# Fewer steps of the weights' conversion in the first batch row of an attention and mixer kernel

## The chip, the core and the metric

The kernel runs on one core of a Trainium2 chip. The metric is the device time of one execution in microseconds (us); 1392.67 us is the median of seven runs before the change (1392.23 to 1396.2). Engine names are those of the profile: PE is the matrix engine, PEld its weight load, DVE the vector engine, ACT the scalar engine, POOL the GpSimd engine, SP the sync engine; SPq and ACTq are DMA issues from SP and ACT.

## The reference

Eight batch rows; in each, eight heads of 576 tokens and width 64. Attention keeps only scores close to the row's maximum, then a mixer follows, first over tokens, then over channels.

```python
scores = q @ k.T / 8                                   # (8, 8, 576, 576)
scores = where(scores >= max(scores) - tau, scores, -1e9)
attn = exp(scores - max); attn /= sum(attn) + 1e-9
x = (attn @ v) -> (8, 576, 512)                        # heads side by side
u = x + (relu(x.T @ w_tok1) @ w_tok2).T                # 576 -> 256 -> 576
out = u + relu(u @ w_ch1) @ w_ch2                      # 512 -> 1536 -> 512
```

The four weights arrive in 64-bit floating point, the rest in 32 bits. The kernel computes in 32 bits, so it must convert the weights on the chip first.

## The kernel before

**Units.** The work on attention is cut into 144 units, 18 for each batch row. A unit is 128 query tokens of a pair of heads (the fifth of every nine units has instead the last 64 tokens of two pairs). One iteration `u` of the main loop does several stages for different units: `scores(u)` (PE, L301) with the row maximum on DVE (`mx`, L306) and the bias on POOL (L307); `norm(u - 1)` (DVE L330, L331; POOL L334); the transposes of the weights of unit `u - 2`; `weigh(u)` (ACT: L316, then the exponential L323); and `values` (PE, L408 and L413, tiles `pv`), every second unit or so.

In batch row 0 the transposes are made on PE (L357, tiles `tr`) and copied out by DVE or ACT (L359, tiles `eT`). In later rows DVE transposes 32 x 32 blocks (L368, tile `T`) and 16 DMAs on SP's queue put the blocks in place (L378, `eT<-T`), one such group for two units, or for the shared unit.

**The mixer.** When a batch row's attention is done, its mixer is pushed to a list of small steps; `fill(share)` takes steps from it into the following row's units, a fixed cost per unit. So rows 1 to 7 have attention and mixer matmuls in one PE queue, and row 0 has attention alone. The steps are: transposes of x (L430), the token mixer (L439, L446, with DVE's addition L450), the channel mixer's first product `ch1` (L468, into a double-buffered PSUM tile that ACT's relu L469 empties) and its second `ch2` (L480, L484).

**The weights' conversion.** The weights come in 31 pieces: 0 to 2 are `w_tok1`, 3 to 6 `w_tok2`, 7 to 18 `w_ch1`, 19 to 30 `w_ch2`. A piece is loaded by SP (L176) into one of four raw buffers, and converted by two ACT instructions (L191, L193), three DVE instructions (L201, L205, L209) and one POOL addition (L215). `weight(n)` issues the next `n` of 94 steps:

```python
for k in range(steps_done, min(steps_done + n, 3 * len(pieces) + 1)):
    i, part = divmod(k, 3)
    if part == 0:
        on_gpsimd(i - 1)
        if i:
            load_piece(i - 1 + NRAW)
    else:
        on_scalar(i + 1, part - 1)
    on_vector(i, part)
```

So each step has one DVE instruction. Every third step has besides the POOL addition of the piece before, and the load of the piece three ahead, which needs the raw buffer that this addition has just read. The two others have an ACT instruction for the next piece. The order on every engine is the program's order; nothing is reordered.

`weight` is called in an iteration after `scores` and `norm` (rows after 0 only), ahead of `weigh(u)`, and behind `weigh(u)`. Row 0 takes the last two calls, and the rows after it take two steps in all three calls, until the 94 are done. `need(i)` issues steps early if a mixer step wants piece `i` and it hasn't been issued.

The loads of q and k (L106) are on SP's queue in row 0 and on ACT's in later rows; v (L114) is always on SP's. `prep` (DVE L283) transposes q and k of a pair of heads.

Of the kernel before, what the change touches and what calls it, by code (L numbers as in the profile page):

```python
# [21 lines left out]
def kernel(  # L22
# [144 lines left out]
    def load_piece(i):  # L167
        if i >= len(pieces):
            return
        dst, src = pieces[i]  # L170
        rows = dst.shape[0]
        n = 1
        for d in dst.shape[1:]:
            n *= d
        raw = raw_at[i % NRAW][0:rows, 0 : n * (2 if wide(i) else 1)].bitcast(src.dtype)
        nc.sync.dma_start(out=like(raw, dst), in_=src)  # L176
        if wide(i):
            words = raw.bitcast(U32).rearrange("p (n w) -> p n w", w=2)
            h2 = work.tile([P, WMAX], F32, tag="o", name=f"h2_{i}")[0:rows, 0:n]
            raws[i] = like(words[:, :, 0], dst), like(words[:, :, 1], dst), like(h2, dst)  # L180
        else:
            raws[i] = like(raw, dst)
# [4 lines left out]
    def on_scalar(i, part):  # L187
        if wide(i):
            lo, hi, h2 = raws[i]
            if part == 0:  # L190
                nc.scalar.activation(out=lo.bitcast(I32), in_=lo, func=AF.Copy, scale=2.0**-29)  # L191
            else:
                nc.scalar.activation(out=h2, in_=hi.bitcast(F32), func=AF.Square)  # L193

    def on_vector(i, part):
        if wide(i):
            dst = pieces[i][0]
            lo, hi, h2 = raws[i]
            bits = dst.bitcast(U32)
            if part == 0:  # L200
                nc.vector.tensor_scalar(  # L201
                    out=bits, in0=hi, scalar1=3, scalar2=0x3FFFFFFF, op0=ALU.logical_shift_left, op1=ALU.bitwise_and
                )
            elif part == 1:
                nc.vector.scalar_tensor_tensor(  # L205
                    out=bits, in0=hi, scalar=0xC0000000, in1=bits, op0=ALU.bitwise_and, op1=ALU.bitwise_or
                )
            else:
                nc.vector.scalar_tensor_tensor(out=dst, in0=h2, scalar=2.0**-30, in1=dst, op0=ALU.is_ge, op1=ALU.mult)  # L209

    def on_gpsimd(i):
        if i >= 0:
            dst = pieces[i][0]
            if wide(i):
                nc.gpsimd.tensor_tensor(out=dst.bitcast(I32), in0=dst.bitcast(I32), in1=raws.pop(i)[0].bitcast(I32), op=ALU.add)  # L215
            else:
                nc.gpsimd.tensor_copy(out=dst, in_=raws.pop(i))
# [5 lines left out]
    def weight(n):  # L223

        nonlocal steps_done
# [9 lines that stand above are left out]
            steps_done = k + 1  # L235
# [39 lines left out]
    def in_blocks(b):  # L275
        return b > 0
# [10 lines left out]
    def scores(u):  # L287
        b, p0, t = units[u]
        sc = [
            (ps_3rd if b == 0 and (2 * u + h) % 3 == 2 else ps_sc).tile([P, 2, MAIN], F32, tag="sc", name=f"sc{h}_{u}") for h in range(2)  # L290
        ]
        if t == SHARED:
            parts = [(b * NP + p0 + i, slice(MAIN, S), slice(64 * i, 64 * i + 64)) for i in range(2)]
        else:
            i, c = divmod(t - (t > SHARED), NI)
            parts = [(b * NP + p0 + i, slice(P * c, P * c + P), slice(0, P))]
        order = [(f, part, h) for f in range(2) for part in parts for h in range(2)]
        for f, (n, cols, rows), h in order if b else sorted(order, key=lambda o: o[2]):
            r = slice(D * h, D * h + D)
            qT, kT = heads[n]  # L300
            nc.tensor.matmul(sc[h][rows, f, 0:HS], lhsT=qT[r, cols], rhs=kT[r, HS * f : HS * f + HS], start=True, stop=True)  # L301
        mx = small.tile([P, 2], F32, tag="mx", name=f"mx_{u}")
        bias = small.tile([P, 2], F32, tag="bias", name=f"bias_{u}")
        for h in range(2):
            c = slice(h, h + 1)
            nc.vector.tensor_reduce(out=mx[:, c], in_=sc[h][:, :, 0:HS], axis=AX.XY, op=ALU.max)  # L306
            nc.gpsimd.tensor_scalar(out=bias[:, c], in0=mx[:, c], scalar1=toff, scalar2=-SCALE, op0=ALU.add, op1=ALU.mult)  # L307
        st[u] = sc, bias
# [18 lines left out]
    def norm(u):  # L327
        e, rs = st[u]
        rr = small.tile([P, 2], F32, tag="rr", name=f"rr_{u}")
        nc.vector.tensor_scalar(out=rr, in0=rs, scalar1=1e-9, scalar2=None, op0=ALU.add)  # L330
        nc.vector.reciprocal(out=rr, in_=rr)  # L331
        for h in range(2):
            eh = e[:, S * h : S * h + S]
            nc.gpsimd.tensor_scalar(out=eh, in0=eh, scalar1=rr[:, h : h + 1], scalar2=1.0, op0=ALU.mult, op1=ALU.mult)  # L334
        st[u] = e

    def group_of(u):

        b, p0, t = units[u]
        if t == SHARED:  # L340
            return (b, p0, "s"), 0, 1
        i, c = divmod(t - (t > SHARED), NI)
        return (b, p0 + i, c // 2), c % 2, 2
# [17 lines left out]
    def turn_blocks(u):  # L361

        key, place, n = group_of(u)
        e = st.pop(u)
        if place == 0:
            Ts[key] = work.tile([P, NK * 2 * P], F32, tag="T", name=f"T_{u}")
        T = Ts[key][:, 0 : NK * n * P]
        nc.vector.transpose(  # L368
            out=T.rearrange("p (a c n x) -> p c a n x", a=4, c=NK, n=n)[:, :, :, place, :],
            in_=e.rearrange("p (c a x) -> p c a x", c=NK, a=4),  # L370
        )
        if place == n - 1:
            del Ts[key]
            eTs[key] = work.tile([P, NK * 2 * P], F32, tag="eT", name=f"eT_{u}")
            w = NK * n * 32
            for a in range(4):
                for i in range(4):
                    nc.sync.dma_start(  # L378
                        out=eTs[key][32 * a : 32 * a + 32, w * i : w * i + w], in_=T[32 * i : 32 * i + 32, w * a : w * a + w]
                    )  # L380
# [151 lines left out]
    b_now = 0  # L532
    LAG = 2
    for u in range(len(units) + LAG + 4):
        on = u < len(units)
        if u == UB:
            late.close()
            ps_mm = ctx.enter_context(tc.tile_pool(name="ps_mm", bufs=2, space=bass.MemoryType.PSUM))
        if on:
            b_now, p0, t = units[u]  # L540
            n = b_now * NP + p0
        w = u - LAG
        back = 0 <= w < len(units)
        if on:
            scores(u)
        if 0 < u <= len(units):
            norm(u - 1)
        if b_now:
            weight(2)
        if back:  # L550
            key, place, many = group_of(w)
            if in_blocks(key[0]):
                turn_blocks(w)
            else:
                for i in range(3):
                    turn(w, i)
            if place == many - 1:
                b, p, c = key
                if c == 0 and p % 2 == 0:
                    split_middle(b * NP + p)  # L560
                if c == "s":
                    split_middle(b * NP + p + 1)
                when = u + (2 if in_blocks(b) else 1)
                due += [(when, b, p + i, c) for i in range(2 if c == "s" else 1)]
        if b_now:
            fill(0.4)
        weight(2 if b_now else 1)
        if on:
            weigh(u)
        elif b_now:  # L570
            fill(0.6)
        weight(2 if b_now else 1)
        if on:
            m = n + 2 + t // 4
            if t < 8 and m < len(pairs):
                load_qk(m, (nc.scalar if b_now else nc.sync,) * 2, t % 4)
                if t % 4 == 3:
                    load_v(m)
            if t == 2:
                prep(n + 1)  # L580
            if t == 7 and n + 2 < len(pairs):
                prep(n + 2)
        while due and due[0][0] <= u:
            _, b, p, c = due.popleft()
            values(b, p, c)
            if p == NP - 1 and c == 1:
                push(b)
# [31 lines left out]
```

## Time and profile before

| | |
|---|---|
| median of 7 runs | 1392.67 us (1392.23 to 1396.2) |
| the profiled execution's own time, and its span | 1393.08 us, 1391.3 us |
| mean granted PE clock | 0.989 |
| PE busy | 1327.6 us (95%), 6866 matmuls |
| DVE, ACT, POOL busy | 585.9 us, 590.5 us, 359.3 us |
| chain that ended last | PE 86%, DVE 6%, DMA 2%, POOL 2%, SPq 2% |
| DMA | 128.34 MB, mean 92 GB/s |

A busy share is an average over stages with different limits. In the profile's picture of 40 slices (34.8 us each) PE is under 90% in the first five slices only. The first scores start at 8.1 us, row 1's first scores at 101.3 us, the first mixer matmuls at 125.5 us, and the last conversion instruction of the weights is POOL's at 197.7 us.

### The profile page before, as it was taken

To read this page: it belongs to the slowest core of one execution; us is meant where nothing else is said; L and a number is where in the kernel's file an instruction comes from. 1 tells how busy PE (TensorE), PEld (TensorE's weight loads), DVE (VectorE), ACT (ScalarE), POOL (GpSimd) and SP (SyncE) were. 2 spreads that over 40 slices of the span, in tenths; PEclk is the share of its full clock that TensorE was granted. 3 is DMA by queue.
4 is the path that set the end of the run, shared out by engine and by line. 5 is a ranking of instruction groups with operands and counts; after the bars stand their busy time and mean duration, and the time that the engine had idled before them with its cause. 6 is when DMAs were issued, how large, how long until landed. Compare 5 with 4: busy or idle time off the path is not lost.

```text
span 1391.3 us, 19515 instructions
## 1 busy us (share of the span) xinstructions
PE 1327.6 (95%) x6866; PEld 831.3 (60%) x6866; DVE 585.9 (42%) x1009; ACT 590.5 (42%) x1328; POOL 359.3 (26%) x683
## 2 busy tenths in 40 slices
PE   5776899999999999999999999999999999999998
PEld 3443465646565566665766567565657566575675
DVE  5789784444444444434243344433333453101000
ACT  5776564544454444443434435353434444120110
POOL 4566563232222222212222222221221222000000
PEclk9997999999999999999999999999999999999999
DMA  6354754443444434433434444443433433300000
GB/s 131 91 121 115 196 139 122 110 119 92 109 116 107 106 86 99 109 83 79 110 84 93 102 96 102 99 104 80 98 92 89 102 77 85 84 8 16 8 8 23
DMA packets 257376, 128.34 MB, mean 92 GB/s; under 512 B 208064, under 2 KB 221376, under 8 KB 257280
## 3 DMA queue, kind: packets, MB, share of 16 engines
q1 hardware_dynamic: 131632, 111.46, 30.5%
q10 hardware_dynamic: 125648, 15.64, 7.1%
q8 instruction: 55, 0.90, 0.3%
q14 instruction: 41, 0.34, 0.1%
HBM read 43.25 MB, written 9.44 MB: 38 GB/s over the span
## 4 chain that ended last, share of the span: by engine, by line
PE 86%; DVE 6%; DMA 2%; POOL 2%; SPq 2%; ACT 1%; issue 1%; ACTq 0%; DVEq 0%; POOLq 0%
PE c L484 27%; PE c L468 26%; PE sc L301 11%; PE pv L413 7%; PE t L439 5%; PE t L446 3%; DVE mx L306 3%; PE pv L408 2%; SPq L378 2%; PE tx L430 1%; PE c L480 1%; PE pv_s L413 1%; DVE T L368 1%; DMA scratch<-in_moe_w_ch_dram 1%; POOL e L334 1%
## 5 line engine op out<-in xcount | busy, mean ns | idle before, releaser
L306 DVE TENSOR_REDUCE mx<-sc 128x1 f32<-128x576 f32 x288 | 204.7, 752 | 525.2 <-PE sc L301 523.2
L468 PE MATMUL c<-xT,wc 128*128 128x256 f32 (+1 forms) x1920 | 399.0, 361 | 1.5 <-ACT g L469 1.4
L484 PE MATMUL c<-wc,g 128*128 128x512 f32 x864 | 389.1, 596 | 0.0
L468 PEld LDWEIGHTS c<-xT,wc 128*128 128x128 f32 x1920 | 334.2, 190 | 71.3 <-issue 28.0
L307 POOL TENSOR_SCALAR bias<-mx,toff 128x1 f32<-128x1 f32 x288 | 80.1, 278 | 814.1 <-DVE mx L306 757.9
L316 ACT ACTIVATE e<-sc,bias 128x576 f32<-128x576 f32 x288 | 199.3, 740 | 158.0 <-POOL bias L307 157.7
L484 PEld LDWEIGHTS c<-wc,g 128*128 128x128 f32 x864 | 157.9, 190 | 175.2 <-issue 173.2
L469 ACT ACTIVATE g<-c 128x256 f32<-128x256 f32 (+1 forms) x240 | 86.9, 362 | 334.3 <-PE c L468 326.9
L334 POOL TENSOR_SCALAR e<-e,rr 128x576 f32<-128x576 f32 x288 | 219.7, 776 | 15.8 <-DVE rr L331 3.8
L323 ACT ACTIVATE e<-e,ntau 128x576 f32<-128x576 f32 x288 | 220.6, 771 | 0.0
L301 PE MATMUL sc<-kT,qT 64*128 64x288 f32 (+1 forms) x1280 | 190.7, 435 | 13.4 <-DVE kT L283 8.1
L368 DVE STREAM_TRANSPOSE T<-e 128x1152 f32<-128x1152 f32 x126 | 172.5, 1369 | 16.2 <-DMA eT<-T 10.0
L301 PEld LDWEIGHTS sc<-kT,qT 64*128 64x128 f32 (+1 forms) x1280 | 103.9, 180 | 90.3 <-issue 47.9
L413 PE MATMUL pv<-eT,lv 128*64 128x256 f32 x1024 | 125.6, 389 | 0.0
L413 PEld LDWEIGHTS pv<-eT,lv 128*64 128x64 f32 x1024 | 75.7, 141 | 39.3 <-issue 4.1
L418 ACT COPY xT<-pv 128x256 f32<-128x256 f32 x64 | 23.8, 372 | 162.0 <-PE pv L413 154.3
L489 DVE COPY o<-c 128x512 f32<-128x512 f32 x36 | 24.5, 680 | 160.8 <-PE c L484 160.8
L446 PE MATMUL t<-w,a 128*128 128x288 f32 x256 | 78.0, 433 | 12.7 <-DVE xT L450 9.6
L439 PE MATMUL t<-x_sb,w 128*128 128x512 f32 x160 | 72.6, 600 | 0.7 <-ACT g L469 0.7
L446 PEld LDWEIGHTS t<-w,a 128*128 128x128 f32 x256 | 46.1, 194 | 40.3 <-DVE xT L450 17.5
L450 DVE TENSOR_TENSOR xT<-xT,t 128x288 f32<-128x288 f32 x64 | 27.9, 440 | 80.4 <-PE t L446 80.2
L323 ACT ACTIVATION_READ_ACCUMULATOR e<-e,ntau 128x1 f32 x288 | 56.4, 196 | 0.0
(48 smaller groups left out, 602.7 us busy)
## 6 DMA issues: line engine op xcount, KB each, us to landing
eT<-T SPq DMA_DIRECT2D x896, 72.0 KB, 2.0
scratch<-in_moe_w_ch_dram SPq DMA_DIRECT2D x24, 512.0 KB, 4.0
lv<-in_v_dram SPq DMA_DIRECT2D x32, 288.0 KB, 3.4
out_dram<-o SPq DMA_DIRECT2D x36, 256.0 KB, 2.2
eT<-T SPq DMA_DIRECT2D x224, 36.0 KB, 1.9
lk<-in_k_dram ACTq DMA_DIRECT2D x108, 72.0 KB, 2.7
lq<-in_q_dram ACTq DMA_DIRECT2D x104, 72.0 KB, 2.1
lq<-in_q_dram SPq DMA_DIRECT2D x24, 72.0 KB, 3.4
```

The costliest lines, as they stand in the source:

```text
L301: nc.tensor.matmul(sc[h][rows, f, 0:HS], lhsT=qT[r, cols], rhs=kT[r, HS * f : HS * f + HS], start=True, stop=True)
L306: nc.vector.tensor_reduce(out=mx[:, c], in_=sc[h][:, :, 0:HS], axis=AX.XY, op=ALU.max)
L316: nc.scalar.activation(out=eh, in_=sc[h][:, :, 0:HS], func=AF.Prelu, bias=bias[:, h : h + 1], scale=SCALE, alpha=STEEP)
L323: nc.scalar.activation(out=eh, in_=eh, func=AF.Exp, bias=ntau, accum_out=rs[:, h : h + 1])
L334: nc.gpsimd.tensor_scalar(out=eh, in0=eh, scalar1=rr[:, h : h + 1], scalar2=1.0, op0=ALU.mult, op1=ALU.mult)
L368: nc.vector.transpose(out=T.rearrange("p (a c n x) -> p c a n x", a=4, c=NK, n=n)[:, :, :, place, :], in_=e.rearrange("p (c a x) -> p c a ...
L413: nc.tensor.matmul(to[r], lhsT=lv[:, j, :], rhs=eT[:, j], start=False, stop=(c == NI - 1), skip_group_check=True)
L439: nc.tensor.matmul(ps, lhsT=w1[:, t, P * m : P * m + P], rhs=x_sb[:, t, :], start=(t == 0), stop=(t == NT - 1))
L446: nc.tensor.matmul(ps, lhsT=s["a"][:, m, P * c : P * c + P], rhs=w2[:, m, HS * f : HS * f + HS], start=(m == 0), stop=(m == NTK - 1))
L468: nc.tensor.matmul(ps, lhsT=wc1[:, j, c, :], rhs=uT[:, c, GR * i : GR * i + n], start=(c == 0), stop=(c == NCC - 1))
L469: nc.scalar.activation(out=s["g"][:, j, 0:n], in_=ps, func=AF.Relu)
L484: nc.tensor.matmul(flat, lhsT=s["g"][:, j, P * t : P * t + P], rhs=wc2[:, j, :], start=False, stop=(j == NJ - 1), skip_group_check=True)
```

## The change

One call of `weight` changes, the one ahead of `weigh(u)`. In row 0 it issued one step in each of the 18 units; now it issues one in units 0, 3, 6, 9, 12 and 15 (`u % 3 == 0` is a truth value, which counts as 1 or 0). The call behind `weigh(u)` still issues one step per unit.

```diff
         if b_now:
             fill(0.4)
-        weight(2 if b_now else 1)
+        weight(2 if b_now else u % 3 == 0)
         if on:
             weigh(u)
         elif b_now:
             fill(0.6)
         weight(2 if b_now else 1)
```

Row 0 so ends with 24 steps issued instead of 36: pieces 0 to 7 have their DVE instructions behind them, not pieces 0 to 11. Rows after 0 still issue six steps per unit. The 94th step is issued in unit 29 instead of unit 27. PE's instructions stand in the same order in both kernels.

## The prediction

> **What bounds the kernel now.** I read the picture of 40 slices first, to see where PE has room at all.
>
> ```profile
> PE   5776899999999999999999999999999999999998
> DVE  5789784444444444434243344433333453101000
> ```
>
> PE is full from the sixth slice on, so an edit is worth what it changes before about 200 us: the time is the moment at which PE is full, plus a queue of matmuls whose order doesn't change. In slices 3 and 4 DVE is the busiest engine. The chain of waits runs in row 0 (8 to 101 us) through PE's scores, DVE's maximum, DVE's copies `eT` and back to PE; between 101 and 185 us it also passes POOL's addition L215, a load into the raw buffers and ACT's L191; from 190 us it is PE alone.
>
> Next, DVE's timeline in row 0 (start, duration, what it did, in brackets the idle time before it). The scores of unit 15 take PE from 86.25 to 87.50.
>
> ```profile
> 83.56 1.42 DVE L306 TENSOR_REDUCE mx<-sc 128x1 f32<-128x576 f32 x2 [2.39 <-PE sc L301]
> ...
> 86.83 0.68 DVE L205 SCALAR_TENSOR_TENSOR wc<-scratch,wc 128x512 uint32<-128x512 uint32 x1
> 87.54 0.69 DVE L209 SCALAR_TENSOR_TENSOR wc<-h,wc 128x512 f32<-128x512 f32 x1
> 88.16 1.41 DVE L306 TENSOR_REDUCE mx<-sc 128x1 f32<-128x576 f32 x2
> ```
>
> Unit 14 has `pv` matmuls ahead of its scores, and DVE idles 2.39 us: conversion there is free. Unit 15 has none; two steps stand ahead of its maximum, which starts 0.6 us late. So a removed step is worth nothing in half of the units.
>
> Then SP's queue and ACT's timeline where the conversion ends.
>
> ```profile
> 165.57 2.69 SPq L176 DMA_DIRECT2D scratch<-in_moe_w_ch_dram  x2
> 168.36 11.01 SPq L378 DMA_DIRECT2D eT<-T  x16
> 179.48 1.50 SPq L176 DMA_DIRECT2D scratch<-in_moe_w_ch_dram  x3
> ```
> ```profile
> 183.49 0.68 ACT L191 ACTIVATE scratch<-scratch 128x512 int32<-128x512 uint32 x1 [4.83 <-DMA scratch<-in_moe_w_ch_dram]
> ...
> 186.30 1.37 ACT L316 ACTIVATE e<-sc,bias 128x576 f32<-128x576 f32 x2
> ```
>
> The loads of pieces 28 to 30 stand behind 16 block DMAs (unit 24's group), whose issue takes 11 us. ACT waits 4.83 us for the first, and the scores of unit 26 (PE, 180.03) reach ACT's L316 only at 186.30. PE loses just 0.97 us, since three `ch1` and a `pv_s` lie between the scores of units 26 and 27.
>
> **Row 0: the gain.** Out of it go 12 steps of 512 columns: by rows such as those above 4 x (0.42 + 0.69 + 0.69) = 7.2 us of DVE, 4 x 1.3 us of POOL, 8 x 0.67 us of ACT (0.55 us apart) and four loads. 7.2 us would be the gain if DVE ended last everywhere. What is on the path:
> - Units 1 to 4. ACT's L193 (16.34) no longer stands ahead of unit 1's L316 (16.90): 0.55 us. At 22.97 L205 and L209 (1.32 us) stand ahead of `prep` and unit 3's maximum (25.65), whose scores are ready at 24.07; one L201 (0.42) takes their place. Iteration 3 then runs the two wider instructions itself (1.37 for 1.1 us). I take 0.8 us of these.
> - Unit 6: L191 (39.53) ahead of L316, and L209 (0.88) ahead of the maximum: 0.6 us.
> - Units 9 and 13: 0.1 us each (maxima at 57.47 and 77.53 against scores ready at 57.28 and 77.11; iteration 12 keeps two steps, but of 288 columns). Unit 15: 0.6 us.
> - Iteration 17: L191 (100.70) delays L316 to 101.27, and with it the scores of unit 18; DVE then has two steps ahead of the maximum at 103.86. Of 0.55 us on ACT and 1.0 us on DVE I take 0.8.
>
> Sum 3.0 us; at least 1.5 (units 9, 13, 15, 18 alone).
>
> **Units 18 to 26: moved as a block.** They run six steps each as before, on pieces numbered four lower, with the same three raw buffers filled ahead, so I move them by the gain. One difference: the load ahead of L191 at 131.53 is then of `w_ch1`; an earlier one of those landed 3.65 us after its issue (109.15), this one took 4.19: 0.5 us more gain. In all -3.5 us.
>
> **Units 27 to 29: the loss.** The 12 DVE steps come back here. As DVE work they cost nothing: PE ends last, and DVE, 45% busy from 200 us, is then as full as it is now in units 25 to 27. Were that cover gone, mx of unit 29 would be some 2 us late. What costs is the order on SP. Pieces 27 to 30, loaded by 181 us before, are now issued in iterations 26 and 27, so that pieces 28 to 30 fall behind unit 26's group of block DMAs. In the times of before:
>
> ```profile
> 184.27 1.97 POOL L334 TENSOR_SCALAR e<-e,rr 128x576 f32<-128x576 f32 x2
> 186.22 3.23 POOL L215 TENSOR_TENSOR wc<-wc,scratch 128x512 int32<-128x512 int32 x2
> ```
>
> That group starts at 186.34. Ahead of it now stands the load of piece 27, which waits for iteration 26's first addition (186.22 + 1.6 = 187.85, as at 165.57 above, where the second load and the group waited for L215): group at 188.35. It takes 10.05 to 11.0 us: load of piece 28 at 198.4 to 199.4, landed 4.0 us later (179.48 to 183.49), at 202.4 to 203.4. ACT has it next, at the end of iteration 27, and reaches it at 196. Behind it on ACT are L193, piece 29's pair, a relu and then unit 28's L316: 2.6 us as in 183.49 to 186.30 (less a copy), so L316 starts at 205.0 to 206.0 instead of 199.16. It empties the scores' PSUM tiles, 0.65 and 1.35 us later.
>
> ```profile
> 195.67 1.24 PE L301 MATMUL sc<-kT,qT 64*128 64x288 f32 x8
> 196.84 3.72 PE L468 MATMUL c<-xT,wc 128*128 128x256 f32 x16
> 200.49 0.65 PE L408 MATMUL pv<-eT,vl 128*64 128x256 f32 x4
> 200.98 1.90 PE L413 MATMUL pv<-eT,lv 128*64 128x256 f32 x16
> 202.80 1.24 PE L301 MATMUL sc<-kT,qT 64*128 64x288 f32 x8
> ```
>
> Here only 7.1 us of matmuls lie between two units' scores. Unit 29's can start at 205.7 and end at 207.3 to 208.3, not 204.04: 3.2 to 4.2 us, I take 3.7. The later steps then have room: unit 29's L316 ends by 212.7 where PE wants the buffers at 214, and `ch2` wants piece 30 at 218 where POOL is done by 216.
>
> **The clock.** That leaves PE empty for about 2.8 us. The two nearest gaps in the trace:
>
> ```profile
> 116.17 0.90 PE L357 MATMUL tr<-ident,e 128*128 128x128 f32 x3 [2.58 <-DVE eT L359]
> ...
> 167.08 2.21 PE L446 MATMUL t<-w,a 128*128 128x288 f32 x8 [2.33 <-DVE xT L450]
> ```
> ```profile
> 116.00:118.00 2.00, 1.82 (x7) 0.50 0.00 0
> 118.00:120.00 2.00, 2.00 (x10) 0.50 0.22 69
> 120.00:122.00 2.00, 2.00 (x12) 0.50 1.13 296
> ```
>
> In the windows (PE busy, matmuls, granted clock) the gap of 2.58 us is followed by 6.6 us at half clock, the one of 3.04 us (107.13) by 3.3, the one of 2.28 (31.83) by 5.5, and the one of 2.33 at 167.08 by none. Half clock costs half of its length where PE is the bound: 0 to 3.3 us. I take 2.5, from the mean of the first two, which are nearest.
>
> The Trainium skill ("TensorE: Matmul & The Clock Gate", HAM oscillation) puts the limit at idle gaps above about 3.4 us. By it 2.8 us would cost no clock and the sum would be +0.2; this trace shows the drop after shorter gaps.
>
> **Sum.** -3.5 + 3.7 + 2.5 = +2.7 us on 1393.08 us, the profiled execution's own time, which is 0.4 us above the median: 1395.4 us as a median. A difference of 0.2% (2.8 us) is about what a measurement of this kernel can tell from no change.
>
> **Rivals.**
> - *The wait finds cover, and the kernel is faster.* If piece 28 lands by 199 us (3.4 us sooner), L316 of unit 28 ends in time for unit 29's scores at 202.80, PE has no gap, and row 0's gain stays: -3.5, 1389.2 us. For it: the same wait of ACT at 183.49 cost PE 0.97 us. Against it: the 2 us of matmuls fewer in unit 28, and the 16 issues, which never took under 10 us between 137 and 190 us. Below this, row 0 could give up to 7.2 us.
> - *The wait without the clock's drop.* As after 167.08: +0.2, 1392.9 us.
> - *Row 0 gives less.* If only units 9, 13, 15 and 18 count, 1.5 us come in, the loss of 6.2 stays: +4.7, 1397.4 us. For it: at the start PE, DVE, ACT and POOL wait for each other, and a gain at one is lost at the next.
> - That the change doesn't do what it says is not open: 18 + 6 = 24 steps by the loop, and the orders on the engines show pieces 0 to 7 ahead of row 1.
>
> **How the numbers follow.** The sum above: 0.50, its own range 1393.4 to 1397.4 by the bounds of wait and clock, so half of it on each side of +0.2%. Covered wait: 0.22, nearly all faster. No drop: 0.13, nearly all the same. Small gain: 0.15, slower. That makes faster 0.22, same 0.38, slower 0.40. The range runs from the covered wait to the small gain with the longer stall: 1388.9 to 1398.6.
>
> **What would show it.** Right: row 1's first scores near 98 us instead of 101.3; seven loads in SP's queue from 179 us on, less the gain, three of them behind the group of unit 26; ACT's L191 waiting 6 us for a load ahead of unit 28's L316; a PE gap of 2 to 4 us ahead of unit 29's scores, with windows of clock 0.5 after it. Wrong: no such gap; row 1's first scores at 101 us; or units 18 to 26 taking longer or shorter than before (with unit 27, 94.3 us from 101.33 to 195.67), which would mean that they don't move as a block.

## The result, and the profile after

The changed kernel takes 1396.29 us (median of 16 runs, 1394.78 to 1401.39) against 1393.08 us before (39 runs beside it): ratio 1.0025, 95% interval 1.0017 to 1.0033, by the ratio 3.5 us slower. The forecast was 1395.4 us, with the ending "slower by over 0.2%" as the likeliest of three. As differences: +2.7 us forecast, +3.5 us measured.

Two profiled executions of the changed kernel were taken. The first lasted 1392.69 us, less than any of the 16 timed runs; the second lasted 1396.31 us, close to the median. The lines below are of the second; the first is named where it differs. Of the kernel before there is a second profile too (1393.46 us). Groups of block DMAs are named as in the prediction, by the iteration that issues them: "unit 24's group" is issued in iteration 24 (for the shared unit 22), "unit 26's group" in iteration 26 (for units 23 and 24).

In the picture of 40 slices (tenths of busy time) of the second profile after, slices 3 to 7 are the ones to compare with those of before:

```profile
PE   6777889999999999999999999999999999999998
DVE  6778885444444443434343444433433453101000
```

DVE has less in slices 3 and 4 (7 and 8 instead of 8 and 9) and more in slices 5 and 7 (8 and 5 instead of 7 and 4): the conversion went from row 0 into the time behind it. PE has more in slice 4 (7 instead of 6) and is full one slice later than it was: slice 6 is an 8. From unit 31 on the two kernels are equal: in each of the four profiles 1172.7 to 1172.8 us lie between the start of unit 31's scores and the end of the span. So the whole account lies in the first 220 us. The starts of the scores (PE L301 in the timeline) cut it in three:

| us from one unit's scores to another's | 5 to 18 | 18 to 26 | 26 to 31 |
|---|---|---|---|
| before, two profiles | 64.26, 64.26 | 78.70, 78.68 | 38.51, 39.86 |
| after, two profiles | 62.88, 63.04 | 77.34, 77.84 | 42.88, 44.25 |

Row 0 gave 1.3 us, units 18 to 26 about 1.1 us, and units 26 to 31 took 4.4 us back: +2.0 us in the mean of two executions each, +3.0 us if the second profile after is taken alone, against 3.5 us between the medians. The last column mixes two things. Unit 26's part of it holds a wait that both kernels have, for the load behind unit 24's group (shown below); from unit 27's scores to unit 31's, where the moved steps and loads lie, it is 29.42 us in both profiles before, and 30.87 and 35.95 us after. (Units 0 to 5 take 26 to 30 us in either kernel, and vary more from run to run than the change could move them.)

Row 0, DVE's timeline around unit 15 (start, duration, what it did, in brackets the idle time before it), second profile after:

```profile
82.47 1.42 DVE L306 TENSOR_REDUCE mx<-sc 128x1 f32<-128x576 f32 x2 [3.11 <-PE sc L301]
...
85.73 0.45 DVE L205 SCALAR_TENSOR_TENSOR w<-scratch,w 128x288 uint32<-128x288 uint32 x1
86.49 1.42 DVE L306 TENSOR_REDUCE mx<-sc 128x1 f32<-128x576 f32 x2 [0.31 <-PE sc L301]
```

One short step stands ahead of the maximum instead of two long ones, and DVE now waits for the scores: unit 15's 0.6 us came in as priced.

SP's queue and ACT's timeline, where the conversion ends:

```profile
176.22 1.50 SPq L176 DMA_DIRECT2D scratch<-in_moe_w_ch_dram  x3
177.77 0.42 SPq L114 DMA_DIRECT2D lv<-in_v_dram  x1
185.52 0.33 SPq L176 DMA_DIRECT2D scratch<-in_moe_w_ch_dram  x1
185.95 11.86 SPq L378 DMA_DIRECT2D eT<-T  x16
197.93 1.50 SPq L176 DMA_DIRECT2D scratch<-in_moe_w_ch_dram  x3
```
```profile
192.30 0.67 ACT L191 ACTIVATE scratch<-scratch 128x512 int32<-128x512 uint32 x1 [4.54 <-DMA scratch<-in_moe_w_ch_dram]
192.88 0.37 ACT L469 ACTIVATE g<-c 128x256 f32<-128x256 f32 x1
...
201.88 0.72 ACT L191 ACTIVATE scratch<-scratch 128x512 int32<-128x512 uint32 x1 [4.75 <-DMA scratch<-in_moe_w_ch_dram]
...
204.64 1.34 ACT L316 ACTIVATE e<-sc,bias 128x576 f32<-128x576 f32 x2
```

Seven loads from 176 us on, the load of piece 27 right ahead of unit 26's group, those of pieces 28 to 30 behind it: the order forecast. ACT waits twice. Its 4.75 us for piece 28 were forecast (6 us), and L316 of unit 28 follows 2.76 us after it. Its 4.54 us for piece 27 were not: this load was issued at 185.52, ahead of the group, but piece 27 was there only 6.8 us later. In the first profile the same load (182.78), with the group behind it too (183.21), landed 4.05 us after its issue, and ACT didn't wait for it; what made it late in the second is not shown. Piece 28 took 4.0 us (197.93 to 201.88) with no group right behind it.

PE's timeline, with both gaps, and the windows (start and end, length, then busy time and number of instructions of PE, PEld, DVE, ACT and POOL; then the granted clock, here 1.00, 0.61, 0.53, the DMA share and GB/s):

```profile
193.29 2.69 PE L468 MATMUL c<-xT,wc 128*128 128x256 f32 x8 [2.59 <-ACT g L469]
195.91 2.19 PE L301 MATMUL sc<-kT,qT 64*128 64x288 f32 x8
...
205.41 1.86 PE L301 MATMUL sc<-kT,qT 64*128 64x288 f32 x8 [1.35 <-ACT e L316]
```
```profile
192.00:194.00 2.00, 0.70 (x3) 0.66 (x4) 2.00 (x3) 1.70 (x4) 2.00 (x3) 1.00 0.18 46
194.00:196.00 2.00, 2.00 (x8) 1.17 (x7) 1.93 (x2) 2.00 (x6) 1.41 (x1) 0.61 0.49 120
196.00:198.00 2.00, 2.00 (x8) 1.09 (x8) 0.69 (x1) 1.13 (x4) 0.00 (x0) 0.53 0.48 120
...
204.00:206.00 2.00, 0.65 (x4) 0.29 (x2) 1.97 (x4) 2.00 (x5) 0.30 (x1) 1.00 0.34 54
206.00:208.00 2.00, 2.00 (x12) 1.36 (x12) 1.90 (x2) 2.00 (x6) 1.10 (x1) 1.00 0.45 111
```

The gap ahead of unit 29's scores, releaser ACT's L316, is there, but it is 1.35 us (0.76 in the first profile), not 2.8, and no window after it shows a lower clock. The half clock follows another gap, 2.59 us behind relu L469, which stood behind the wait for piece 27.

In the first profile after, the gap with half clock behind it lies one unit earlier:

```profile
163.60 12.26 SPq L378 DMA_DIRECT2D eT<-T  x16
175.97 1.50 SPq L176 DMA_DIRECT2D scratch<-in_moe_w_ch_dram  x3
180.06 0.68 ACT L191 ACTIVATE scratch<-scratch 128x512 int32<-128x512 uint32 x1 [5.40 <-DMA scratch<-in_moe_w_ch_dram]
182.44 3.59 PE L468 MATMUL c<-xT,wc 128*128 128x256 f32 x8 [2.29 <-ACT g L469]
```
```profile
182.00:184.00 2.00, 1.56 (x4) 1.29 (x5) 1.97 (x4) 2.00 (x5) 1.21 (x2) 0.57 1.13 214
184.00:186.00 2.00, 2.00 (x8) 1.27 (x6) 1.90 (x2) 1.99 (x6) 0.94 (x1) 0.57 0.91 304
```

That is the load of piece 24 behind unit 24's group, at the place that piece 28 had before. PE's gap there was 0.97 and 2.32 us in the two profiles before, 2.29 and 0.17 us in the two after: it varies from one execution to the next in either kernel, and is not what the change added.

### The profile page after: what moved, and what is told of

Read it like the earlier page. It is cut to its first block, busy times and chain, and to the rows that moved or that the text cites. A ratio compares the mean times of both kernels' runs of the same rounds, so it can differ in the third digit from the quotient of the medians.

```text
span 1390.9 us, 19529 instructions
## 1 busy us (share of the span) xinstructions
PE 1325.8 (95%) x6866; PEld 831.6 (60%) x6866; DVE 589.2 (42%) x1009; ACT 590.1 (42%) x1328; POOL 360.4 (26%) x683
## 4 chain that ended last, share of the span: by engine, by line
PE 85%; DVE 5%; DMA 3%; ACT 2%; SPq 2%; POOL 1%; issue 1%; ACTq 0%; DVEq 0%
PE c L484 27%; PE c L468 25%; PE sc L301 11%; PE pv L413 7%; PE t L439 5%; PE t L446 3%; PE pv L408 2%; DVE mx L306 2%; SPq L378 1%; PE tx L430 1%; DMA scratch<-in_moe_w_ch_dram 1%; PE c L480 1%; PE pv_s L413 1%; DVE T L368 1%; DMA eT<-T 1%
## 5 line engine op out<-in xcount | busy, mean ns | idle before, releaser
L316 ACT ACTIVATE e<-sc,bias 128x576 f32<-128x576 f32 x288 | 199.1, 739 | 153.5 <-POOL bias L307 153.1
L469 ACT ACTIVATE g<-c 128x256 f32<-128x256 f32 (+1 forms) x240 | 86.9, 362 | 331.5 <-PE c L468 326.7
L301 PE MATMUL sc<-kT,qT 64*128 64x288 f32 (+1 forms) x1280 | 189.5, 434 | 18.6 <-ACT e L316 10.5
L301 PEld LDWEIGHTS sc<-kT,qT 64*128 64x128 f32 (+1 forms) x1280 | 104.0, 179 | 93.8 <-issue 47.7
```

The lines of the kernel that those rows point to most:

```text
L316: nc.scalar.activation(out=eh, in_=sc[h][:, :, 0:HS], func=AF.Prelu, bias=bias[:, h : h + 1], scale=SCALE, alpha=STEEP)
L469: nc.scalar.activation(out=s["g"][:, j, 0:n], in_=ps, func=AF.Relu)
```

## The experiments

Times are medians; ratios are to the kernel before, with 95% intervals. In the kernels that leave loads out, lines after L176 have numbers higher by one. The first theory is that of the forecast: the loss is made of loads that stand in SP's queue behind a group of block DMAs. Its rival: it is the moved conversion steps' own work on DVE, ACT and POOL.

**Second profiles of both kernels, unchanged.**

> The changed kernel unaltered, for a second profile: the first one was taken in an execution of 1392.69 us, while the median of the others is 1396.29 us. Theory A (the loads of pieces 28 to 30 behind unit 26's block DMAs, then the clock): in an execution near 1396 us units 0 to 26 are 3 to 5 us ahead of before, and 6 to 8 us are lost between the scores of units 28 and 30, with a PE gap of 2 to 4 us ahead of unit 29's scores and half clock after it. Theory B (the gain is lost already at units 23 to 26, where SP's queue does not move up with the other engines): the gap and the half clock stand ahead of unit 27, as in the first profile (2.29 us at 182.4), and are longer than there.

> The kernel before unaltered, for a second profile. Both theories: row 1's first scores at 101.3 us, the scores of unit 28 at 195.7 us and of unit 30 at 209.7 us within 1.5 us, since its executions lie between 1390.0 and 1396.7 us; a later unit 28 goes with more half clock between 100 and 185 us.

Measured: 1396.31 and 1393.46 us; their lines are above. The changed kernel fits neither theory in full: unit 26's scores are 1.6 to 2.5 us ahead of before, not 3 to 5; 3.0 us are lost between the scores of units 28 and 30, not 6 to 8; and the larger gap, with the half clock, lies ahead of unit 28. Before came as expected in its three starts (100.38, 196.05 and 210.09 us). Its second profile shows that before pays for its late load as well: the load of piece 28 stands behind unit 24's group, and PE's timeline has there

```profile
186.27 1.99 PE L468 MATMUL c<-xT,wc 128*128 128x256 f32 x8 [2.32 <-ACT g L469]
```

where the first profile had 0.97 us. The prediction had taken the 0.97 for the price of that wait.

**The last three loads left out, in both kernels.** The loads of pieces 28 to 30 are not issued, and the conversion takes what the raw buffers hold.

```diff
-        nc.sync.dma_start(out=like(raw, dst), in_=src)
+        if i < 28:
+            nc.sync.dma_start(out=like(raw, dst), in_=src)
```

> The changed kernel without the loads of pieces 28 to 30, whose weights are then stale; all other instructions stay. Theory A: ACT's wait ahead of unit 28's L316 and the PE gap ahead of unit 29 go, and with them 5 to 6.5 us: 1389.5 to 1391 us, 2 to 3.5 us under before. Theory B: these loads cost little (0.76 us in the first profile), 1395 to 1396 us.

> The control: the kernel before without the loads of pieces 28 to 30. There they stand behind the group of unit 24, and ACT waits 4.83 us for the first of them ahead of unit 26. Theory A: PE loses 0.97 us to that, so 1392 us. Theory B: the wait of this place costs 2 to 3 us on average, clock included, so 1390 to 1391 us.

Measured: from the changed kernel 1390.58 us, ratio 0.9984 (0.9976 to 0.9993); from the one before 1390.92 us, ratio 0.9986 (0.9977 to 0.9996). Without these three loads the kernels are equal. In ratios the loads cost the changed kernel 1.0025 - 0.9984 = 0.0041, or 5.7 us, and the kernel before 0.0014, or 2.0 us. The difference of 3.7 us (the intervals leave it 2 us of room either way) is as large as the slowdown of 3.5 us. The two prices are not of one place: in the changed kernel the three loads stand behind unit 26's group, in the kernel before behind unit 24's, where the changed kernel has pieces 24 to 26, which this run still loads. Units 26 to 31 take 39.37 us (24 steps) and 37.36 us (36 steps): 2 us more with no wait for these three loads (a PE gap of 1.02 us behind piece 27's load is in it), and row 0's gain pays for it.

**Piece 27 too; and all loads from piece 11 on.** The same edit with 27, in the changed kernel, and with 11 in both.

> The changed kernel without the loads of pieces 27 to 30 (stale weights), one load more than in the run without 28 to 30 (1390.58 us). Theory A: PE's gap ahead of unit 28 (2.59 us and 2 us of half clock in the second profile, 1.02 us in the run without 28 to 30) comes from piece 27, so 1 to 2.5 us less, 1388 to 1389.5 us. Theory B: no change, 1390 to 1391 us.

Measured: 1391.11 us, ratio 0.998 (0.997 to 0.9991), against 0.9984 with only 28 to 30 left out. That is the second theory's time. With pieces 28 to 30 already left out, piece 27's load can't be shown to cost anything of its own: 0.6 us, inside the intervals. A likely reason, which no run separates: an early stall in unit 28 is time in which the loads behind the group come nearer, so two gaps in one profile need not be two costs.

> The kernel before without the loads of pieces 11 to 30 (those weights are stale), so that rows 1 and 2 hold no load of a weight; every conversion instruction stays. It is the baseline for the next kernel. Both theories: ACT's waits for loads between 108 and 185 us go, 12 to 18 us by the sum of those waits, of which PE gets back 5 to 9: 1384 to 1388 us.

> The changed kernel without the same loads. Theory A (all of the loss is waits for loads, that of piece 27, issued just ahead of unit 26's block DMAs, included): with no loads in row 1 the change is a pure gain of row 0, 1.5 to 3 us under the kernel without loads before. Theory B (the 12 conversion steps themselves cost in units 27 to 29, on DVE, ACT or POOL): equal to it or up to 3 us above it.

Measured: 1387.85 us, ratio 0.9953 (0.9937 to 0.9969), with 36 steps in row 0, and 1387.17 us, ratio 0.9947 (0.9929 to 0.9964), with 24. So with no wait for weights in units 18 to 30 at all, 24 steps and 36 are equal within the intervals: the change is no pure gain of row 0 (0.7 us, where the first theory said 1.5 to 3), and the gain is returned by the steps themselves. Units 5 to 18 take 62.69 instead of 64.28 us, units 18 to 26 73.95 instead of 74.57 us, units 26 to 31 39.46 instead of 37.28 us. DVE's, POOL's and PE's timelines of the kernel with 24 steps and no loads from piece 11 on show the cause:

```profile
182.95 1.42 DVE L307 TENSOR_REDUCE mx<-sc 128x1 f32<-128x576 f32 x2
...
187.49 1.52 DVE L202 TENSOR_SCALAR wc<-scratch 128x512 uint32<-128x512 uint32 x1
189.04 1.67 DVE L206 SCALAR_TENSOR_TENSOR wc<-scratch,wc 128x512 uint32<-128x512 uint32 x1
190.82 0.69 DVE L210 SCALAR_TENSOR_TENSOR wc<-h,wc 128x512 f32<-128x512 f32 x1
191.43 1.42 DVE L307 TENSOR_REDUCE mx<-sc 128x1 f32<-128x576 f32 x2
...
193.04 0.41 DVE L202 TENSOR_SCALAR wc<-scratch 128x512 uint32<-128x512 uint32 x1
193.48 0.70 DVE L206 SCALAR_TENSOR_TENSOR wc<-scratch,wc 128x512 uint32<-128x512 uint32 x1
...
199.91 1.42 DVE L307 TENSOR_REDUCE mx<-sc 128x1 f32<-128x576 f32 x2
```
```profile
186.92 3.24 POOL L216 TENSOR_TENSOR wc<-wc,scratch 128x512 int32<-128x512 int32 x2
```
```profile
186.57 1.24 PE L302 MATMUL sc<-kT,qT 64*128 64x288 f32 x8
...
193.72 1.83 PE L302 MATMUL sc<-kT,qT 64*128 64x288 f32 x8
...
201.85 0.75 PE L302 MATMUL sc<-kT,qT 64*128 64x288 f32 x2 [0.55 <-ACT e L317]
202.79 1.23 PE L302 MATMUL sc<-kT,qT 64*128 64x288 f32 x6 [0.20 <-ACT e L317]
```

With six steps in an iteration DVE has no idle time between the maxima of units 27, 28 and 29, and they come 8.48 us apart (182.95, 191.43, 199.91). PE needs 6.55 us from unit 27's scores to unit 28's (180.02 to 186.57) and 7.15 to unit 29's. So DVE falls behind by 1.3 to 1.9 us a unit, the maximum of unit 29 starts 6.2 us after its scores (1.27 us in the kernel with 36 steps, 197.25 to 198.52), and unit 30's scores wait for ACT, which waits for that chain. From unit 29's scores to unit 31's PE takes 17.90 us instead of 15.74. With 36 steps all but four are done before unit 27, and in units 24 to 26 PE takes 9.8, 8.9 and 7.9 us (36 steps, pieces 28 to 30 not loaded), which covers nearly all of the same DVE work.

**30 steps in row 0.** The value that lies between the two kernels.

```diff
-        weight(2 if b_now else 1)
+        weight(2 if b_now else u % 3 != 2)
```

> The kernel before with 30 steps in row 0 (the call ahead of weigh gives one step in two units of three). The 94th step is then issued in unit 28, and only the load of piece 30 falls behind unit 26's block DMAs, but ACT has it next at the end of iteration 27, where the changed kernel has piece 28. Theory A: the wait ahead of unit 28's L316 is nearly the same as in the changed kernel, and row 0 gains half: 1395 to 1397 us, no better than 24 steps. Theory B (loss in proportion to the steps moved): half of the change, 1394 to 1395 us.

Measured: 1393.58 us, ratio 0.9999 (0.9983 to 1.0014): no different from 36 steps, under both theories' times, and its interval ends below the 1.0017 at which that of 24 steps begins. Units 5 to 18 take 62.69 us, so all of row 0's gain in them is there with half of the steps moved, not half of it. Its profile has the same gap ahead of unit 29, 2.05 us behind L316, but units 26 to 31 at 41.4 us instead of 43 to 44. Why one load behind the group costs nothing on balance, with that gap, was not separated further.

**Loads issued by POOL.** A load stands right behind the POOL addition that frees its buffer, and no block DMAs of SP's queue ahead of it. Nothing is left out.

```diff
-        nc.sync.dma_start(out=like(raw, dst), in_=src)
+        (nc.gpsimd if i >= 15 else nc.sync).dma_start(out=like(raw, dst), in_=src)
```

> 36 steps in row 0, but the loads of pieces 15 to 30 are issued by POOL, right behind its additions, instead of by SP, so that none stands behind a group of block DMAs. Theory A (the loss is made of loads waiting behind block groups): as with the loads of pieces 28 to 30 left out, 2 to 3 us under the kernel before, 1390.5 to 1391.5; ACT's wait of 4.83 us ahead of unit 26's L316 goes below 1 us. Theory B (the conversion's own work in rows after 0 is what costs, whatever the queue): as before, 1393.5. If an issue on POOL holds up POOL's own additions and biases by 1 us each, up to 5 us slower.

> 24 steps in row 0, and the loads of pieces 15 to 30 issued by POOL instead of SP. Theory A: the waits ahead of units 28 and 29 go, 5 to 6 us under the changed kernel, 1390 to 1391.5, within 1 us of the kernel with 36 steps and the same queue; units 26 to 31 take about 39.4 us instead of 43 to 44. Theory B: 1395 to 1396. If an issue on POOL costs POOL 1 us each, up to 5 us more in either theory.

Measured: 36 steps 1392.72 us, ratio 0.9994 (0.9986 to 1.0003); 24 steps 1393.52 us, ratio 1.0002 (0.9994 to 1.0011). Changing only the queue took 0.0023, or 3.2 us, off the changed kernel and 0.0006, or 0.8 us, off the one before (its interval holds no change too), and closed the distance between them from 3.5 to 1.1 us. Units 26 to 31 take 40.2 us with 24 steps (39.4 expected) and 37.28 us with 36. The expected times, up to 1391.5 us, were missed by 2.0 us with 24 steps and by 1.2 us with 36. With 36 steps ACT's wait ahead of unit 26's L316 is 3.03 us, not under 1, but PE no longer loses by it (7.86 us from unit 26's scores to unit 27's, 9.10 and 10.45 in the profiles before). POOL's timeline of the kernel with 24 steps shows what an issue costs there:

```profile
185.51 0.58 POOL L176 DMA_DIRECT2D scratch<-in_moe_w_ch_dram  x1 [0.30 <-POOL wc L215]
186.12 1.30 POOL L215 TENSOR_TENSOR wc<-wc,scratch 128x512 int32<-128x512 int32 x1
187.71 0.55 POOL L176 DMA_DIRECT2D scratch<-in_moe_w_ch_dram  x1 [0.30 <-POOL wc L215]
188.75 0.26 POOL L307 TENSOR_SCALAR bias<-mx,toff 128x1 f32<-128x1 f32 x1 [0.50 <-DVE mx L306]
```

Each takes 0.85 to 1.05 us of POOL with the idle time before it, and these loads land 4.7 us after the issue (median); those of the changed kernel on SP's queue took 4.1 and 4.3 us in its two profiles. So the last run moved only the four loads that the change had moved beside and behind unit 26's group (`i >= 27`).

> 24 steps in row 0, and only the loads of pieces 27 to 30 (the four beside and behind unit 26's group) issued by POOL; 15 to 26 stay on SP. Theory A (these four loads behind the group are the loss, and the dozen other issues on POOL cost what the kernel with sixteen lost): close to the changed kernel with the loads left out, 1391 to 1392.5, so 1 to 2.5 us under the kernel before; units 26 to 31 take 39.4 to 40.5 us. Theory B (a load issued by POOL lands later or delays POOL as much as the wait behind the group did, or the loss lies elsewhere): 1393.5 or more.

Measured: 1392.76 us, ratio 1.0004 (0.9994 to 1.0014): 0.0021, or 2.9 us, under the changed kernel and equal to the kernel before. Units 26 to 31 take 39.95 us. Of ACT's two waits 2.47 and 1.39 us are left:

```profile
189.88 0.71 ACT L191 ACTIVATE scratch<-scratch 128x512 int32<-128x512 uint32 x1 [2.47 <-DMA scratch<-in_moe_w_ch_dram]
...
197.26 0.67 ACT L191 ACTIVATE scratch<-scratch 128x512 int32<-128x512 uint32 x1 [1.39 <-DMA scratch<-in_moe_w_ch_dram]
```

The expected 1391 to 1392.5 us were missed by a little. The theory of the waits is confirmed in the main thing: with the 24 steps kept and four loads moved to another queue, the loss is gone within the interval. None of the versions that convert all weights beats the kernel before by more than its interval. The Trainium skill ("DMA: Bandwidth & Descriptors", Rules for kernel authors) says that spreading DMAs over the issuing engines brings no bandwidth and only saves a sequencer's issue time; here that issue time, 11.86 us of block DMAs ahead of a load, was what counted.

**48 steps in row 0.** The other direction.

```diff
-        weight(2 if b_now else 1)
+        weight(2 if b_now else 1 + (u % 3 != 2))
```

> 48 steps in row 0 (two steps ahead of every unit but each third, one behind each). The last loads are then issued in iteration 23, ahead of the shared unit's group, and ACT's conversion of piece 28 comes a unit or more earlier. Theory A: row 0 is 1.5 to 2.5 us longer (units 5 to 18 at 65.5 to 66.5 us instead of 64.2), the wait for piece 28 (2.6 us as timed) goes, and with it some of the steps' own cost: 1391.5 to 1393.5. Theory B (each step moved out of row 0 is a gain, the waits have cover): 2 us or more above the kernel before, 1395.5 or more.

Measured: 1400.87 us (1396.55 to 1407.17), ratio 1.0053 (1.0035 to 1.0071): 7.4 us slower. This missed the first theory's 1391.5 to 1393.5 and lies where the second put it, at 1395.5 or more. But the late wait, which the second took to be covered, did go: units 26 to 31 take 37.28 us, as with the loads left out. Row 0 was underpriced: units 5 to 18 take 66.95 us, 2.7 more than before, where 1.5 to 2.5 was expected. Its profiled execution (1397.01 us) is near the quickest of its runs and starts unit 31 at 222.46 us against 218.54 in the first profile before: 1.9 us up to unit 5, 2.7 to unit 18, and 0.7 given back behind it. What makes its median another 3.9 us longer is in no profile and stays open.

## Why the prediction was right, point by point

The time came out 0.9 us above the forecast and in the likeliest case: a gain in row 0, given back by loads behind unit 26's group. That part of the mechanism is shown: leave those three loads out and no slowdown is left; issue them and piece 27's from another queue and it is gone within the interval. That the time came so near is in part luck: three terms of the sum were off, and partly cancelled. The range given for the sum, 1393.4 to 1397.4 us, is not what its bounds of wait (3.2 to 4.2) and clock (0 to 3.3) add up to: with the gain of 3.5 they give -0.3 to +4.0, or 1392.4 to 1396.7 us.

- *Row 0 and units 18 to 26: -3.5 forecast, -2.4 in the profiles.* Units 6, 9, 13 and 15 (1.4 us forecast) gave 1.2 to 1.4. Units 18 to 26 gave 0.8 to 1.4, where iteration 17 (0.8) and the earlier `w_ch1` load (0.5) were forecast at 1.3. The 0.8 of units 1 to 4 can't be seen: the start-up varies by several us in either kernel.
- *The 12 DVE steps "cost nothing": wrong.* This is the step that failed most. The cover it named, "as full as it is now in units 25 to 27", is not the same in units 27 to 29: there PE takes 6.6 to 7.2 us a unit, not the 7.9 to 9.8 of units 24 to 26, and DVE's six steps, maximum and transposes need 8.48. With no loads in the way it costs 2.2 us (39.46 against 37.28). The text priced the loss of that cover at 2 us of lateness for unit 29's maximum; it is 4.9 us there (6.2 against 1.27), and 2.4 and 1.7 us in the two profiles of the changed kernel itself (3.70 and 2.95 against 1.27). How much of the changed kernel's time is the steps' own can't be told: a stall for a load gives DVE time to catch up, and the measured prices (-2.4, +5.7 for the loads, +2.2 for the steps) add up to more than 3.5.
- *The wait for piece 28: mechanism right, place and size off.* Without the loads of pieces 28 to 30 no slowdown is left, and in the changed kernel they cost 5.7 us, where stall and clock together were forecast at 6.2. But the 3.7 us of stall were put ahead of unit 29 as one piece. In the second profile, whose time is the typical one, a gap of 2.59 us ahead of unit 28 comes first, through relu L469, because piece 27 was usable only 6.8 us after its issue, and 1.35 us are left for unit 29. The 0.97 us that the text took for the price of the wait behind unit 24's group was one execution's: the other had 2.32, and without the three loads the kernel before is 2.0 us faster. The changed kernel has that wait too, for piece 24; whether it pays as much for it on average, no run separates.
- *The clock: 2.5 us forecast after the gap ahead of unit 29.* After that gap there was none. After the gap of 2.59 us ahead of unit 28 the windows at 194 to 198 us show 0.61 and 0.53 of full clock: some 1.7 us (4 us x 0.43). In the first profile no window from 186 to 220 us is under 1.00; its two of 0.57 follow the wait for piece 24, which is not the change's.
- *Rivals.* The covered wait didn't occur: neither profile of the changed kernel is without a gap. "No drop of the clock" describes unit 29 but not unit 28. "Row 0 gives less" was half right, and its 1397.4 us is about as near to the result as the forecast is.
- *Units 18 to 26 as a block.* The condition named for being wrong, as it was put, came true: from unit 18's scores to unit 28's the two profiles after take 95.9 and 96.2 us, not 94.3. But the second profile before takes 95.7 us, so the sign tells little. Up to unit 26 the units moved together and gained what was priced for iteration 17 and the load. What comes on top differs: in the first profile after it is the wait for piece 24 between the scores of units 26 and 27 (12.01 us, where before took 9.10 and 10.45), in the second the wait for piece 27 between those of units 27 and 28 (10.10 us, 6.55 before).

## What to carry to other kernels

Work moved out of a stage is free only where the receiving engine has room in those very units: compare its time per unit with the bound engine's time per unit, not its share over a slice. A load that is issued by a queue in program order inherits all that stands ahead of it there, so moving a compute step by some units can put its load behind a long group of small DMAs; look at what the queue does then. One profile is one execution: the same wait cost PE 0.97 us in one and 2.32 us in the next, and a price read from one of them is one draw. And a gain of 2 to 3 us at one end and a larger loss at the other are both real here, so a difference of 3 us has to be found by taking one suspect out of both kernels.

## What the runs showed of the hardware

- The granted clock doesn't follow the length of a gap alone. A gap of 2.29 us (first profile after, ahead of 182.44) was followed by two windows of 0.57, one of 2.32 us (second profile before, ahead of 186.27) by windows of 1.00, and so was one of 2.05 us with 30 steps in row 0. The Trainium skill ("TensorE: Matmul & The Clock Gate", HAM oscillation) names idle gaps above about 3.4 us; drops after 2.29 and 2.59 us lie below that.
- L201 takes 0.41 us or 1.52 us and L205 0.70 or 1.67 us for the same 128x512 tile. The long ones (184.26 and 185.81 in the second profile after) lie beside POOL's two additions L215 (183.69, 3.25 us), though L209 at 183.69, beside the same additions, takes 0.64 us. By subtraction, without these 2.1 us in an iteration DVE's 8.48 us would be 6.4, less than PE's unit.
- A load of 512 KB with 16 block DMAs issued right behind it landed anything from 3.47 to 6.97 us after its issue (both in the second profile before, issued at 135.88 and 153.05); piece 27's took 4.05 us in the first profile after and 6.70 in the second. Piece 28's, issued right behind such a group, took 3.93 to 4.00 us in the two profiles. What decides is not shown.
